# Keys and values of a token tile as one 1280-column product over three PSUM banks, with a block of MLP weights loaded ahead of later tokens and a longer estimate for late transposes

## The chip, the cores and the metric

The kernel runs on one core of one Trainium2 chip. The metric is the time of one execution in microseconds (us), measured on the device; lower is better. Several executions are timed, and medians with their ranges are given. The profile of one execution comes from the hardware profiler. Its span is shorter than the timed figure of the same run (266.6 against 268.37 us for the kernel before).

## The reference

A layer norm feeds two branches, and both are added to the input (S = 2048 tokens, D = 640, 32 heads of 20, F = 1536):

```
xn  = layernorm(x)
# A: linear attention; the features are softmax(p) and softmax(-p) over the 20 channels of a head
q, k, v = split(xn @ wqkv)
pq, pk  = q @ w_phi, k @ w_phi                      # per head
phi     = concat(softmax(p), softmax(-p))
o       = (phi_q @ (phi_k^T v)) / (phi_q . sum(phi_k) + 1e-6)
a       = o @ wo
# B: gated MLP
b       = (silu(xn @ w1) * (xn @ w3)) @ w2
out     = x + a + b
```

## The kernel before

Tokens stand in 16 tiles of 128. A scheduler written in Python runs while the program is built: each piece of work ("a product", "an evacuation", "a DMA") has an estimated duration; the pieces come from twelve streams; the piece that could start first goes next. So each engine gets one fixed order of instructions, made from estimates. The chip then runs each engine's list in order and waits on semaphores where the estimates were too optimistic. Any edit of a cost, or of a piece of work, can reorder everything that follows.

Three terms recur. Each matmul comes with a weight load (PEld in the profile) of its stationary tile, 128 x 128 values by which its columns are multiplied. Its result goes to PSUM, which the program treats as eight banks of 512 columns. An evacuation copies the result out of a bank, which frees the bank for the next product.

The key weights are first folded with w_phi (`fold_mm`), so that one product of xn gives the key features before the exponentials. V and K had a weight tensor each, and each product of a tile filled two banks of 320 columns:

```python
    Wkp = new("Wkp", [128, DC, D], bf, RKV)
    wv = new("wv", [128, DC, D], bf, RKV + 6400)
...
    def proj(t, w, k):
        for q in range(2):
            for i in range(DC):                      # DC = 5 blocks of 128 rows
                mm(bank(k + q, 320), xnT[:, i, t * 128:(t + 1) * 128],
                   w[:, i, 320 * q:320 * q + 320], i == 0, i == DC - 1)
...
    def v_tile(t, k):
        proj(t, wv, k)                               # then one ScalarE copy of 640 columns
...
    def k_features(t, k):
        proj(t, Wkp, k)                              # then two ScalarE exponentials of 640 columns
```

Of the first loads, these go out last, on one queue and in this order; `w13(a, b)` loads columns a to b of w1 and then of w3:

```python
        w13(0, 512)
        P.dma("SP", phi_s[:], phi_t)
        P.dma("SP", wqkT[:, DC:2 * DC, :], A_wqkv[:, D:2 * D], True)
        load_x(4, 8)
        load_x(8, 12)
        w13(512, 1024)
```

The scheduler's estimate of a DMA that transposes (`turn`), from its issue to its landing, ends with this line. After 80 us such transposes are those of the query features (tile `EqT`) and of the attention output (`oT`):

```python
                o.end = self.bus + (2.3 if turn and t > 80 else 1.6 if turn else 1.3 if t < 4.5 else 1.9)
```

The softmax here doesn't subtract the row's maximum and nothing guards it: scores larger than these inputs give would overflow.

## Time and profile before

| | before |
|---|---|
| time, median of 3 | 268.77 us (268.58 to 268.81) |
| span of the profiled run | 266.6 us |
| TensorE (PE) busy | 262.1 us, 1951 matmuls |
| VectorE, ScalarE, GpSimd busy | 182.9, 107.4, 95.6 us |
| PE stalls over 30 ns, after the start-up | 0.55 us at 23.5 us and 0.20 us at 125.7 us |

From the page of the profile: each engine's busy time with its share of the span and its count of instructions; the share of each of 40 slices in which PE is busy; the granted clock of PE in the same slices, in tenths (9 is 90% or more); and the chain of work that ended last.

```profile
span 266.6 us, 4819 instructions
...
PE 262.1 (98%) x1951; PEld 162.1 (61%) x1951; DVE 182.9 (69%) x312; ACT 107.4 (40%) x227; POOL 95.6 (36%) x107
...
PE   7999999999999999999999999999999999999996
...
PEclk9999999999999999999999999999999999999999
...
PE PS L104 90%; SPq L116 5%; DMA w_s<-in_B_w_dram 4%; DVE xres L104 0%
```

PE bounds the kernel. The chain, though, is not PE throughout: 4% of the span is a load of MLP weights. (The profile drops buffer numbers: `w_s` is w1 or w3, and w2.) In order of time (start, duration; "issue" is a moment in which nothing visible is waited for), the load is followed by PE to nearly the end:

```profile
14.78 9.38 DMA w_s<-in_B_w_dram
24.15 0.14 issue
24.29 101.68 PE PS L104 x839
125.97 0.04 issue
126.00 138.34 PE PS L104 x968
```

The timeline of PE just there (start, duration, what ran, and in brackets the idle time before it) shows where the chain leaves PE:

```profile
22.66 1.24 PE L104 MATMUL PS<-xnT,w_s 128*128 128x512 bf16 x5
24.29 1.24 PE L104 MATMUL PS<-xnT,w_s 128*128 128x512 bf16 x5 [0.39 <-DMA w_s<-in_B_w_dram]
25.36 0.48 PE L104 MATMUL PS<-BDc,wqkT 128*128 128x140 bf16 x6
25.68 2.32 PE L104 MATMUL PS<-xnT,w_s 128*128 128x512 bf16 x10
```

Five matmuls on w1 run, and the five on w3 wait for their weights. The five would follow at 22.66 + 5 x 0.216 = 23.74 us; they start at 24.29. That is 0.55 us, more than the 0.39 in brackets, because the end of a matmul is modelled with its pipeline behind it. For the same reason I measure PE by the distance from one matmul's start to the next one's. It was 216 ns at 512 columns, 136 at 320 and 56 at 128, which is columns/2.4 plus 2.7 ns by these medians; whatever is left over by 30 ns or more I call a stall. (Some matmul records are missing from a trace. Such a hole shows as exactly one matmul's time too much and is not counted.)

The waits by pair (who waited for whom, in total us, number, longest) name both stalls of the table, the first seen on PE and the second on its weight loads:

```profile
PE PS L104 <- DMA w_s<-in_B_w_dram: 0.4, 1, 0.4
PEld PS L104 <- DMA EqT<-eqt: 0.4, 1, 0.4
```

Groups by shape (count, busy us, mean ns of one, idle before). The product changed here is the last two lines:

```profile
L104 PE MATMUL PS<-xnT,w_s 128*128 128x512 bf16 x480 | 108.6, 379 | 0.4 <-DMA w_s<-in_B_w_dram 0.4
...
L104 PE MATMUL PS<-wv,xnT 128*128 128x320 bf16 x160 | 24.4, 299 | 0.1
L104 PE MATMUL PS<-Wkp,xnT 128*128 128x320 bf16 x160 | 23.9, 299 | 0.0
```

And the stage in which V and K are made (stretch, then its length and the busy time of PE, weight loads, DVE, ACT and POOL, each with its count; then the granted clock, the DMA engines' share and their GB/s): the other engines are 83% busy or more, but PE has no gap.

```profile
27.80:76.10 48.30, 48.30 (x351) 32.86 (x350) 45.38 (x72) 41.59 (x62) 40.17 (x44) 1.00 0.48 110
```

### The profile page before, as it was taken

What the parts mean: (1) busy time and instruction counts of PE and PEld (TensorE: products, weight loads), DVE (VectorE), ACT (ScalarE), POOL (GpSimd) and SP (SyncE); (2) the same over time, 40 slices, a digit from 0 to 9 for tenths busy, and PEclk for the clock granted to TensorE, in tenths of its full rate; (3) what the DMA queues carried; (4) which work ended last, traced back from release to release, by engine and by line L of the source; (5) the groups of instructions that cost most, each with busy time, mean ns of one, the idle gap of its engine ahead of it and who ended that gap; (6) DMA issues with size and microseconds to landing.
All of it is one profiled execution on the core that took longest, in us unless ns stands there. A gap on an engine that the chain in (4) does not pass through costs nothing.

```text
span 266.6 us, 4819 instructions
## 1 busy us (share of the span) xinstructions
PE 262.1 (98%) x1951; PEld 162.1 (61%) x1951; DVE 182.9 (69%) x312; ACT 107.4 (40%) x227; POOL 95.6 (36%) x107
## 2 busy tenths in 40 slices
PE   7999999999999999999999999999999999999996
PEld 3754666766766756556465655466565746777773
DVE  4567899999777497778767677969775857212112
ACT  5546688898871325332251314451414220000000
POOL 4211289898999032522207030617030430000000
PEclk9999999999999999999999999999999999999999
DMA  7996045962400773619503543061825074331211
GB/s 223 277 316 173 1 105 108 324 85 49 125 0 2 188 247 72 131 28 130 128 0 70 114 85 69 10 128 35 148 52 128 0 126 84 76 98 49 87 38 49
DMA packets 62742, 27.73 MB, mean 104 GB/s; under 512 B 49920, under 2 KB 62720, under 8 KB 62720
## 3 DMA queue, kind: packets, MB, share of 16 engines
q1 hardware_dynamic: 62576, 27.26, 44.4%
q8 instruction: 15, 0.25, 0.4%
q10 hardware_dynamic: 144, 0.16, 0.2%
q14 instruction: 7, 0.06, 0.1%
HBM read 12.81 MB, written 2.62 MB: 58 GB/s over the span
## 4 chain that ended last, share of the span: by engine, by line
PE 90%; SPq 5%; DMA 4%; issue 0%; DVE 0%
PE PS L104 90%; SPq L116 5%; DMA w_s<-in_B_w_dram 4%; DVE xres L104 0%
## 5 line engine op out<-in xcount | busy, mean ns | idle before, releaser
L104 PE MATMUL PS<-xnT,w_s 128*128 128x512 bf16 x480 | 108.6, 379 | 0.4 <-DMA w_s<-in_B_w_dram 0.4
L104 PEld LDWEIGHTS PS<-xnT,w_s 128*128 128x128 bf16 x480 | 46.2, 98 | 51.3 <-DVE Wkp L104 0.9
L104 POOL TENSOR_TENSOR eqt<-eqt,rS 128x600 bf16<-128x600 bf16 (+1 forms) x32 | 41.0, 1304 | 90.8 <-DVE rS L104 90.8
L104 ACT ACTIVATE th<-PS 128x512 f32<-128x512 f32 x48 | 28.6, 595 | 74.0 <-PE PS L104 73.9
L104 PE MATMUL PS<-w_s,hT 128*128 128x320 bf16 (+2 forms) x384 | 54.9, 299 | 0.0
L104 DVE SCALAR_TENSOR_TENSOR t<-th,PS 128x512 bf16<-128x512 f32 x48 | 32.5, 677 | 31.6 <-ACT th L104 31.5
L104 PEld LDWEIGHTS PS<-w_s,hT 128*128 128x128 bf16 x384 | 37.1, 98 | 15.1
L104 POOL TENSOR_TENSOR ekt<-ekt,rS 128x640 bf16<-128x640 bf16 x32 | 39.7, 1273 | 3.9 <-DVE rS L104 3.9
L104 ACT ACTIVATE eqt<-PS 128x240 bf16<-128x240 f32 (+1 forms) x96 | 27.2, 348 | 26.0 <-PE PS L104 24.1
L104 DVE TENSOR_TENSOR xres<-PS,xres 128x640 bf16<-128x640 f32 (+2 forms) x17 | 13.3, 782 | 34.6 <-PE PS L104 34.6
L104 DVE SCALAR_TENSOR_TENSOR hT<-t,PS 128x512 bf16<-128x512 bf16 x48 | 33.0, 687 | 2.0 <-PE PS L104 0.4
L104 ACT ACTIVATE ekt<-PS 128x640 bf16<-128x640 f32 x32 | 22.3, 703 | 7.0 <-PE PS L104 6.4
L104 DVE TENSOR_REDUCE S<-ekt 128x64 f32<-128x1280 bf16 x16 | 23.2, 1452 | 2.2 <-ACT ekt L104 2.2
L104 PE MATMUL PS<-wo_s,oT 128*128 128x320 bf16 (+2 forms) x160 | 24.5, 299 | 0.0
L104 PE MATMUL PS<-wv,xnT 128*128 128x320 bf16 x160 | 24.4, 299 | 0.1
L104 PE MATMUL PS<-Wqp,xnT 128*128 128x360 bf16 (+1 forms) x160 | 24.3, 299 | 0.0
L104 DVE TENSOR_REDUCE S<-eqt 128x66 f32<-128x1320 bf16 x16 | 24.2, 1513 | 0.0
L104 PE MATMUL PS<-Wkp,xnT 128*128 128x320 bf16 x160 | 23.9, 299 | 0.0
L104 PEld LDWEIGHTS PS<-Wqp,xnT 128*128 128x128 bf16 x160 | 15.2, 98 | 7.6
L104 PEld LDWEIGHTS PS<-wv,xnT 128*128 128x128 bf16 x160 | 15.4, 98 | 6.4 <-ACT xnT L104 0.3
L104 PEld LDWEIGHTS PS<-Wkp,xnT 128*128 128x128 bf16 x160 | 15.4, 98 | 6.1
L104 PEld LDWEIGHTS PS<-wo_s,oT 128*128 128x128 bf16 x160 | 15.3, 98 | 6.0
(52 smaller groups left out, 156.7 us busy)
## 6 DMA issues: line engine op xcount, KB each, us to landing
w_s<-in_B_w_dram SPq DMA_DIRECT2D x6, 640.0 KB, 7.2
xres<-in_A_x_dram SPq DMA_DIRECT2D x16, 160.0 KB, 2.5
out_dram<-xres SPq DMA_DIRECT2D x15, 160.0 KB, 1.8
x_tok<-in_A_x_dram SPq DMA_DIRECT2D x3, 640.0 KB, 4.5
w_s<-in_B_w_dram SPq DMA_DIRECT2D x1, 1920.0 KB, 8.8
wo_s<-in_A_wo_dram SPq DMA_DIRECT2D x1, 800.0 KB, 4.7
wv<-in_A_wqkv_dram SPq DMA_DIRECT2D x2, 320.0 KB, 4.3
x_tok<-in_A_x_dram SPq DMA_DIRECT2D x3, 160.0 KB, 2.6
```

Of the source, the lines that this page charges most:

```text
L104: o = _Op(eng, lambda: m(*args, **kw), r, w, cost)
L116: o = _Op(eng, lambda: m(out, in_), self.regions(in_), self.regions(out), nbytes, True)
```

## The change

The intent is fewer matmuls for the same columns, and MLP weights in time. V and K weights become one tensor of 1280 columns. For tiles 4 to 15 the product is cut at bank limits, 512, 512 and 256: 15 matmuls in place of 20. Tiles 0 to 3 have their V early and keep a product for K alone, now 512 + 128. A piece of work may now take any run of free banks, not only an aligned pair. Columns 512 to 1023 of w1 and w3 go ahead of x tiles 8 to 11. And the scheduler's estimate for late transposes grows by 0.4 us.

```diff
-                o.end = self.bus + (2.3 if turn and t > 80 else ...)
+                o.end = self.bus + (2.7 if turn and t > 80 else ...)
...
-    Wkp = new("Wkp", [128, DC, D], bf, RKV)
-    wv = new("wv", [128, DC, D], bf, RKV + 6400)
+    WVK = new("WVK", [128, DC, 2 * D], bf, RKV)
...
         load_x(4, 8)
+        w13(512, 1024)
         load_x(8, 12)
-        w13(512, 1024)
...
     def k_features(t, k):
-        proj(t, Wkp, k)
+        for q, lo, hi in ((0, 0, 512), (1, 512, D)):
+            for i in range(DC):
+                mm(bank(k + q, hi - lo), xnT[...], WVK[:, i, D + lo:D + hi], i == 0, i == DC - 1)
+        k_exps(t, 512 * k)
+
+    def vk_features(t, k):
+        for q, lo, hi in ((0, 0, 512), (1, 512, 1024), (2, 1024, 2 * D)):
+            for i in range(DC):
+                mm(bank(k + q, hi - lo), xnT[...], WVK[:, i, lo:hi], i == 0, i == DC - 1)
+        act(v2[...], PS[:, 512 * k:512 * k + D]..., ACT.Copy)
+        k_exps(t, 512 * k + D)
...
-        return min(range(0, 8, n), key=free_at)
+        return min(range(0, 9 - n), key=free_at)
...
-            yield lambda t=t: k_features(t, banks(2))
...
-            if t >= 4:
-                yield v(t)
...
+            if t < 4:
+                yield lambda t=t: k_features(t, banks(2))
+            else:
+                yield lambda t=t: vk_features(t, banks(3))
```

More of the change, by code (lines that the diff above doesn't have):

```diff
@@ L182, in commit @@
                 self.bus = max(self.bus, t + 0.5) + o.cost / rate
-                o.end = self.bus + (2.3 if turn and t > 80 else 1.6 if turn else 1.3 if t < 4.5 else 1.9)
+                o.end = self.bus + (2.7 if turn and t > 80 else 1.6 if turn else 1.3 if t < 4.5 else 1.9)
             else:
@@ L419, in first_loads @@
         for a, b in ((0, 2), (2, 4), (4, DC)):
-            P.dma("SP", wv[:, a:b, :], wqkv_t[:, a:b, 2 * D:3 * D])
+            P.dma("SP", WVK[:, a:b, 0:D], wqkv_t[:, a:b, 2 * D:3 * D])
         load_x(3, 4)
@@ L533, in fold_mm @@
                     first[q] = False
-        dst = (Wqp, Wkp)[which]
-        evac(dst[:, dc, :].rearrange("p (b c) -> p b c", c=320), bank2(k, 320))
-    def proj(t, w, k):
-        for q in range(2):
-            for i in range(DC):
-                mm(bank(k + q, 320), xnT[:, i, t * 128:(t + 1) * 128],
-                   w[:, i, 320 * q:320 * q + 320], i == 0, i == DC - 1)
+        dst = Wqp[:, dc, :] if which == 0 else WVK[:, dc, D:2 * D]
+        evac(dst.rearrange("p (b c) -> p b c", c=320), bank2(k, 320))
     def v_out(t, q, k):
@@ L552, in v_half @@
         for i in range(lo, hi):
-            mm(bank(k, 320), xnT[:, i, t * 128:(t + 1) * 128], wv[:, i, 320 * q:320 * q + 320],
+            mm(bank(k, 320), xnT[:, i, t * 128:(t + 1) * 128], WVK[:, i, 320 * q:320 * q + 320],
                i == 0, i == DC - 1)
@@ L560, in v_first @@
             for q in range(2):
-                mm(bank(k + q, 320), xnT[:, i, 0:128], wv[:, i, 320 * q:320 * q + 320], i == 0, i == DC - 1)
+                mm(bank(k + q, 320), xnT[:, i, 0:128], WVK[:, i, 320 * q:320 * q + 320], i == 0, i == DC - 1)
         if hi == DC:
@@ L564, in v_first, with k_exps @@
             v_out(0, 1, k + 1)
-    def v_tile(t, k):
-        proj(t, wv, k)
-        pv = bank2(k, 320).rearrange("p b (h c) -> p b h c", c=DH)
-        act(v2[:, t, :].rearrange("p (b h c) -> p b h c", b=2, c=21)[:, :, :, 0:DH], pv, ACT.Copy)
-    def k_features(t, k):
-        proj(t, Wkp, k)
-        o = ekt[:, t, :].rearrange("p (b h s f) -> p b h s f", b=2, s=2, f=DH)
-        for sg in range(2):
-            act(o[:, :, :, sg, :], bank2(k, 320).rearrange("p b (h f) -> p b h f", f=DH), ACT.Exp,
-                1.0 if sg == 0 else -1.0)
+    def k_exps(t, c):
+        o = ekt[:, t, :].rearrange("p (h s f) -> p h s f", s=2, f=DH)
+        i = PS[:, c:c + D].rearrange("p (h f) -> p h f", f=DH)
+        for sg in range(2):
+            act(o[:, :, sg, :], i, ACT.Exp, 1.0 if sg == 0 else -1.0)
+    def k_features(t, k):
+        for q, lo, hi in ((0, 0, 512), (1, 512, D)):
+            for i in range(DC):
+                mm(bank(k + q, hi - lo), xnT[:, i, t * 128:(t + 1) * 128], WVK[:, i, D + lo:D + hi],
+                   i == 0, i == DC - 1)
+        k_exps(t, 512 * k)
+    def vk_features(t, k):
+        for q, lo, hi in ((0, 0, 512), (1, 512, 1024), (2, 1024, 2 * D)):
+            for i in range(DC):
+                mm(bank(k + q, hi - lo), xnT[:, i, t * 128:(t + 1) * 128], WVK[:, i, lo:hi], i == 0, i == DC - 1)
+        act(v2[:, t, :].rearrange("p (h c) -> p h c", c=21)[:, :, 0:DH],
+            PS[:, 512 * k:512 * k + D].rearrange("p (h c) -> p h c", c=DH), ACT.Copy)
+        k_exps(t, 512 * k + D)
     def q_features(t, k):
@@ L813, in attention @@
     def attention():
-        def v(t):
-            return lambda: v_tile(t, banks(2))
         yield warm_up
@@ L832, in attention @@
                 yield None
-            yield lambda t=t: k_features(t, banks(2))
-            done["k"] = t + 1
-            if t >= 4:
-                yield v(t)
-            done["v"] = t + 1
+            if t < 4:
+                yield lambda t=t: k_features(t, banks(2))
+            else:
+                yield lambda t=t: vk_features(t, banks(3))
+            done["k"] = done["v"] = t + 1
             if 9 <= t < 14:
```

## The prediction

> **What bounds the kernel.** TensorE. The page gives PE 262.1 of 266.6 us busy (98%), the granted clock is 1.00 in every stretch, and the chain of waits is PE work from 24.29 us to the last output tile (two PE pieces, 101.7 and 138.3 us). VectorE (183), ScalarE (107) and GpSimd (96) have slack over the whole span. In the V/K stage (27.8 to 76.1 us, view of busy time by stretch) they do not: DVE 45.4, ACT 41.6, POOL 40.2 of 48.3 us; but PE is still busy for all 48.30, because MLP products fill its gaps.
>
> Inside PE, I take start-to-start distances of successive matmuls: 512 columns 216 ns, 320 columns 136, 128 columns 56. That is columns/2.4 GHz plus 2.5 to 2.7 ns, as the Trainium skill's page "TensorE: Matmul & The Clock Gate" (section "Wait — 56ns, not 53.3ns?") has it; a new stationary tile for every matmul costs nothing more. All columns together take 254.0 us at 2.4 GHz; the small overheads sum to 5.3 us over 1951 matmuls. All other PE loss after the first 7 us is two stalls: 0.55 us at 23.5 us (waiting for w3 columns 512-1023, which land at 24.15, behind x tiles 8-11, which land at 19.37) and 0.20 us at 125.7 us (a transposed query tile, EqT).
>
> **What the change does.**
> 1. V and K of tiles 4-15: 20 matmuls of 320 columns become 15 (512, 512, 256). Columns are unchanged. Five fewer per tile, 12 tiles: 60 x 2.65 ns = 0.16 us. PE time of a tile goes from 2.72 us to 2.70.
> 2. K of tiles 0-3 as 512+128 in place of 320+320: same count and columns, nothing.
> 3. Evacuation: the same three ScalarE instructions of 640 columns per tile (0.71 + 2 x 0.72 us). They now come as one 2.15 us group after one product, over three banks. The middle bank is held longer; 3 + 3 + 2 banks still let a second V/K product or an MLP pair run. Nothing on balance, with a small risk of a stall.
> 4. The load order: w1/w3 columns 512-1023 go ahead of 640 KB of x. From the landings 17.58 (x 4-7), 19.37 (x 8-11), 22.43, 24.15 us, w3 should land about 1.8 us earlier, near 22.3, and the stall of 0.55 us goes. x tiles 8-11 land near 24; their statistics start at 34.9, so that is free.
> 5. The scheduling model assumes DMA transposes after 80 us land 0.4 us later. The query stage is then ordered differently; the 0.20 us stall at 125.7 may go (I count 0.1).
>
> All of 1, 4 and 5 are on the critical path, as PE is. Sum: -0.16 - 0.55 - 0.1 = -0.8 us. The order of the whole program after 20 us is recomputed, so I allow +0.15 us for new short stalls. The first 20 us and the tail (last matmul at 264.1, then add and store) do not change.
>
> **Predicted: 268.1 us**, 267.5 to 269.1 (8 in 10). Faster by over 2%: 0.01; within 2%: 0.97; slower by over 2%: 0.02.
>
> **What would show it.** (1) 1891 matmuls, V/K groups with 512 and 256 columns at 216 and 109 ns. (4) No PE gap near 23.5 us; w3's second load landing near 22.3. (3) PE still fully busy from 28 to 76 us. (5) No PE wait on EqT. PE busy near 262 us and a span near 265.9.
>
> **What would make it wrong.** The V/K stage turning ScalarE-bound: the three-bank group held up by ScalarE, PE stalling for a bank; a new order of the query stage with DMA waits on EqT or oT; or K's later evacuation delaying the last key normalisation, so that the K-V sum starts late and PE runs out of MLP work.

## The result and the profile after

| | before | after |
|---|---|---|
| time, median of 6 | 268.79 us (268.20 to 269.00) | 267.64 us (267.37 to 268.11) |
| ratio, after to before | | 0.9962 (95%: 0.9949 to 0.9975) |
| span of the profiled run | 266.6 us | 265.9 us |
| PE busy, matmuls | 262.1 us, 1951 | 262.1 us, 1891 |

A ratio here is the mean time of one kernel's fast runs over that of the other's fast runs of the same rounds, so it is not quite the ratio of the medians. It says 0.38% faster, about 1.0 us; the predicted gain was 0.7 us, and 267.64 lies inside the predicted 267.5 to 269.1.

From the page of the changed kernel, the lines that answer to those of before:

```profile
span 265.9 us, 4695 instructions
...
PE 262.1 (99%) x1891; PEld 155.9 (59%) x1891; DVE 183.9 (69%) x313; ACT 106.3 (40%) x226; POOL 95.9 (36%) x107
...
PE   7999999999999999999999999999999999999996
...
PE PS L104 96%; DMA x_tok<-in_A_x_dram 1%; DVE bst L104 1%; DVE x_tok L104 0%; DVE mv L104 0%; POOL rstd L104 0%; DVE xres L104 0%
```

(This page has no row of the clock; 512-column matmuls were 216 ns apart, as before.) The load of MLP weights is gone from the chain, which is now PE from the start-up to the end. Note what does not show the gain: PE was busy for 262.1 us before and is busy for 262.1 us after, and its row of 40 slices is the same digit for digit. That equality is partly chance: in the first 20 us PE was busy for 18.22 us before and 18.56 after, and from there on for 243.91 and 243.56. The Trainium skill, on the page "Trainium Kernel Development and Optimization" (section "Performance Expectations"), calls matmul busy time a bad metric for how close a kernel is to roofline (the peak rate), because matmuls are pipelined. Here, too, it misled: 0.7 us of span went, and the sum of busy time did not move.

PE's timeline at the place of the first stall (the two groups of five are now one group of ten, without idle time before it):

```profile
22.31 0.60 PE L104 MATMUL PS<-BDc,wqkT 128*128 128x140 bf16 x8
22.75 2.32 PE L104 MATMUL PS<-xnT,w_s 128*128 128x512 bf16 x10
24.90 0.48 PE L104 MATMUL PS<-BDc,wqkT 128*128 128x140 bf16 x6
25.22 2.99 PE L104 MATMUL PS<-WVK,xnT 128*128 128x512 bf16 x20
```

The second w3 load landed at 24.15 us before and lands at 22.93 now. The groups by shape show the new product: 140 matmuls of 512 columns (20 of them for K alone, tiles 0 to 3) and 60 of 256, 216 and 109 ns apart.

```profile
L104 PE MATMUL PS<-xnT,w_s 128*128 128x512 bf16 x480 | 108.2, 379 | 0.0
...
L104 PE MATMUL PS<-WVK,xnT 128*128 128x512 bf16 x140 | 32.9, 379 | 0.0
...
L104 PE MATMUL PS<-WVK,xnT 128*128 128x256 bf16 x60 | 8.5, 273 | 0.0
```

The V/K stage is as full as before, with 58 matmuls fewer in the same stretch, and the waits by pair hold no DMA on EqT. One new wait is on the fold of the key weights:

```profile
27.80:76.10 48.30, 48.30 (x293) 26.49 (x292) 44.57 (x69) 41.64 (x64) 41.96 (x47) 1.00 0.47 110
```

```profile
PEld PS L104 <- ACT WVK L104: 0.4, 1, 0.4
```

(The first fence is the view of busy time by stretch, the second the view of waits.) On PE that wait costs 0.10 us, at 25.87 us: the first K product is reached before the fold of the last 128 rows is out of PSUM.

### The profile page after: what moved, and what is told of

It is laid out like the page before. It is cut to its first block, busy times and chain, and to the rows that moved or that the text cites. A ratio compares the mean times of both kernels' runs of the same rounds, so it can differ in the third digit from the quotient of the medians.

```text
span 265.9 us, 4695 instructions
## 1 busy us (share of the span) xinstructions
PE 262.1 (99%) x1891; PEld 155.9 (59%) x1891; DVE 183.9 (69%) x313; ACT 106.3 (40%) x226; POOL 95.9 (36%) x107
## 4 chain that ended last, share of the span: by engine, by line
PE 96%; DVE 1%; DMA 1%; POOL 0%; issue 0%
PE PS L104 96%; DMA x_tok<-in_A_x_dram 1%; DVE bst L104 1%; DVE x_tok L104 0%; DVE mv L104 0%; POOL rstd L104 0%; DVE xres L104 0%
## 5 line engine op out<-in xcount | busy, mean ns | idle before, releaser
L104 PE MATMUL PS<-WVK,xnT 128*128 128x512 bf16 (+3 forms) x260 | 45.6, 330 | 0.1
L104 PEld LDWEIGHTS PS<-WVK,xnT 128*128 128x128 bf16 x260 | 24.2, 98 | 19.4 <-ACT WVK L104 0.4
L104 ACT ACTIVATE ekt<-PS 128x640 bf16<-128x640 f32 x32 | 22.3, 703 | 1.3 <-PE PS L104 0.8
L104 DVE RECIPROCAL rS<-S 128x64 f32<-128x64 f32 (+1 forms) x32 | 17.9, 560 | 1.1
L104 DVE TENSOR_TENSOR o_tok<-PS,g_s 128x360 bf16<-128x360 f32 (+1 forms) x32 | 15.7, 491 | 1.1
```

The lines of the kernel that those rows point to most:

```text
L104: o = _Op(eng, lambda: m(*args, **kw), r, w, cost)
```

## The experiments

**How the traces are compared.** Every program here has the same work up to the last of the twenty TensorE transposes of the start-up, and that comes at 10.65 to 13.72 us, depending on the run. So I take PE from the start of that transpose to the start of the last matmul, and subtract the stalls of 30 ns or more found in between. What stays is the base: columns plus the fixed cost of each matmul, plus waits too short to count.

Theory "stalls": the gain is a smaller base (fewer matmuls) plus named PE stalls that went. Rival "product": the three-bank product itself is worth more than its 60 matmuls, or the stalls are absorbed later. Rival "reordering": a luckier order of the whole program.

**1. Load order alone** (kernel before; no compute instruction changes place).

```diff
         load_x(4, 8)
+        w13(512, 1024)
         load_x(8, 12)
-        w13(512, 1024)
```

> The kernel before with only the load order changed (MLP columns 512-1023 ahead of x tiles 8-11); the order of every compute engine's instructions is unchanged. Theory 'stalls' (the gain is the removal of named PE stalls): the 0.55 us stall near 23.5 us goes, the 0.20 us wait on EqT near 125 us stays, 1951 matmuls stay; 0.55 us faster than before, near 268.2 us. Rival 'product' (the gain is the three-bank product, the stall is absorbed later): the stall goes but time stays within 0.2 us of before.

Measured: 268.62 us (267.83 to 270.05), ratio 1.0005 (0.9979 to 1.0031). The time expected, 0.55 us faster and near 268.2 us, did not come; the interval is 0.7 us wide to each side and just holds it, so timing neither confirms nor excludes it. The trace is clearer: w3 lands at 22.52 us, there is no stall near 23.5 us, one of 0.12 us on EqT at 125.2 us is left, and the base is that of before (table below). PE has no idle time where the stall was:

```profile
22.75 2.32 PE L104 MATMUL PS<-xnT,w_s 128*128 128x512 bf16 x10
```

**2. Load order alone put back** (changed kernel; again no compute instruction changes place).

> The changed kernel with only the load order put back; the order of the compute engines' instructions is that of the changed kernel. Theory 'stalls': the stall near 23.5 us comes back at 0.5 to 0.6 us and time rises by 0.55 us over the changed kernel, near 268.2 us. Rival 'product': the stall is absorbed, within 0.2 us of the changed kernel.

Measured: 268.35 us (267.55 to 269.01) beside 267.81 for the changed kernel. The medians differ by 0.54 us, as expected, but the ranges overlap, and so do the ratios to before, 0.9978 (0.9953 to 1.0003) and 0.9959 (0.9938 to 0.9980). The profiled run shows a stall of only 0.10 us: w3 landed at 24.30, while PE itself was late, with the last start-up transpose at 11.28 us in place of 10.67. The stall is the difference of two moving times. That was not expected, so the trace of this run does not confirm the stall of 0.5 to 0.6 us.

**3. The load made later** (kernel before).

```diff
         load_x(8, 12)
+        load_x(12, 16)
+        P.pending[-1].cost = 0      # not seen by the scheduler, so that the order is kept
         w13(512, 1024)
```

> The kernel before with 640 KB more ahead of the MLP columns 512-1023: x tiles 12-15 are loaded once before them (and again later, as before, with the same data); the order of all compute instructions is kept. Theory 'stalls': the load's lateness passes one to one into PE time: w1 and w3 land about 1.8 us later, the stall near 23.5 us grows from 0.55 to 2.0 to 2.6 us and time by 1.5 to 2.1 us over before. Rival 'absorbed': later stages have room, time grows by less than half of that.

Measured: 270.53 us (269.72 to 271.11), ratio 1.0060 (1.0030 to 1.0089), 1.7 us over the median before. PE's timeline:

```profile
22.59 0.79 PE L104 MATMUL PS<-BDc,wqkT 128*128 128x140 bf16 x12
24.54 1.24 PE L104 MATMUL PS<-xnT,w_s 128*128 128x512 bf16 x5 [1.16 <-DVE Wkp L104]
26.29 1.24 PE L104 MATMUL PS<-xnT,w_s 128*128 128x512 bf16 x5 [0.51 <-DMA w_s<-in_B_w_dram]
```

The two gaps cost 1.33 and 0.68 us of start-to-start distance, 2.00 in all, at the lower end of the 2.0 to 2.6 expected. (The first is put down to DVE, which had long been done; the w1 load landed at 24.41 us, 0.13 before the start.) Lateness of this load passes into the time; nothing later absorbs it.

**4. The product alone** (load order and estimate as before).

> The kernel before with only the 1280-column product and its three-bank allocation; old load order, old 2.3 us assumption for late transposes. Theory 'stalls': 60 matmuls fewer save 0.16 us; the stall near 23.5 us stays at 0.55 us (order up to there is the same); the order made with 2.3 us plans waits on EqT near 111, 171 and 192 us, which I expect at 0.2 to 1.0 us in all on the chip; net between 0.1 us faster and 0.7 us slower than before. Rival 'product': 0.5 us or more faster than before.

Measured: 269.36 us (268.35 to 270.38), ratio 1.0031 (1.0007 to 1.0054): slower than before. The rival "product" falls. The profiled run, with 268.35 us the fastest of the six, had no stall on w3 (it landed at 23.30 us) but one of 0.77 us on EqT at 190.8 us:

```profile
188.87 2.32 PE L104 MATMUL PS<-xnT,w_s 128*128 128x512 bf16 x10
191.79 0.48 PE L104 MATMUL PS<-KVc,EqT 128*128 128x63 bf16 x11 [0.60 <-DMA EqT<-eqt]
```

The planned waits at 111 and 171 us did not show.

**5. The changed kernel with the old estimate for late transposes.**

```diff
-                o.end = self.bus + (2.7 if turn and t > 80 else ...)
+                o.end = self.bus + (2.3 if turn and t > 80 else ...)
```

> The changed kernel with the assumption for late transposes put back to 2.3 us: same product, same load order. Theory 'stalls': waits of PE on EqT come back near 111, 171 and 192 us, 0.2 to 1.0 us in all, so it is slower than the changed kernel by that much and near 268.0 to 268.6 us; no stall at 23.5 us. Rival 'the assumption does not matter': within 0.1 us of the changed kernel, no wait on EqT.

Measured: 268.75 us (268.49 to 270.38), ratio 1.0014 (0.9991 to 1.0036), so 0.9 to 1.1 us over the changed kernel's medians (267.81 and 267.64), about the upper end of the 0.2 to 1.0 us expected, and a little over the 268.0 to 268.6 us. The trace shows the cause, the same as in experiment 4:

```profile
189.53 2.32 PE L104 MATMUL PS<-xnT,w_s 128*128 128x512 bf16 x10
192.56 0.49 PE L104 MATMUL PS<-KVc,EqT 128*128 128x63 bf16 x11 [0.71 <-DMA EqT<-eqt]
```

The stall measures 0.88 us from start to start. With the larger estimate the order is another, and the traces of the changed kernel have no wait on EqT. One number of the diff decides whether the change gains 1.0 us or ties with before.

**6. That estimate alone** (kernel before).

> The kernel before with only the 2.7 us assumption for late DMA transposes, so the query stage is ordered anew. Theory 'stalls': stall near 23.5 us stays at 0.55; the 0.20 us wait on EqT goes or shrinks; 0.0 to 0.2 us faster than before. Rival 'reordering' (the new order of the query stage is what gained): 0.5 us or more faster.

Measured: 268.49 us (267.82 to 269.28), ratio 0.9993 (0.9973 to 1.0013): no difference resolved, though the interval still reaches a gain of 0.7 us. The trace speaks against "reordering": the base is that of before (252.68 us in the table below), and the wait on EqT, expected to shrink, is 0.20 us in this order too. And the profiled run had waits on both halves of the MLP load, 0.73 and 0.68 us, far over the 0.55 expected:

```profile
23.45 1.24 PE L104 MATMUL PS<-xnT,w_s 128*128 128x512 bf16 x5 [0.57 <-DMA w_s<-in_B_w_dram]
25.21 1.24 PE L104 MATMUL PS<-xnT,w_s 128*128 128x512 bf16 x5 [0.51 <-DMA w_s<-in_B_w_dram]
```

**7. Many more matmuls** (changed kernel; columns, banks, evacuations and the order of all other work kept).

```diff
-        for q, lo, hi in ((0, 0, 512), (1, 512, 1024), (2, 1024, 2 * D)):
+        for lo in range(0, 2 * D, 128):
             for i in range(DC):
-                mm(bank(k + q, hi - lo), xnT[...], WVK[:, i, lo:hi], i == 0, i == DC - 1)
+                mm(PS[:, 512 * k + lo:512 * k + lo + 128], xnT[...], WVK[:, i, lo:lo + 128],
+                   i == 0, i == DC - 1, cost=...)      # the same estimate per column as before
```

> The changed kernel with the 1280 columns of V and K of tiles 4-15 in ten pieces of 128 columns, 50 matmuls per tile in place of 15, 420 more in all; same banks, same evacuations, same order of all other instructions. Theory 'fixed cost per matmul of 2.65 ns': 420 x 2.65 = 1.1 us slower than the changed kernel, 128-column matmuls 56 ns apart. [...]

The expectation set this against a rival, "weight loads", by which a new stationary tile for each matmul sets the pace. One weight load takes 98 ns in the traces, so 600 matmuls would come 42 ns later each, 25 us in all (an estimate from these traces).

Measured: the base rises from 252.48 to 253.53 us, 1.05 us over 420 matmuls, 2.5 ns each. The matmuls of 128 columns of tiles 4 to 15 come 56 ns apart (597 distances, longest 56) although each has a new stationary tile. The rival "weight loads" falls.

```profile
L104 PE MATMUL PS<-WVK,xnT 128*128 128x128 bf16 x615 | 36.0, 219 | 0.0
```

(Groups by shape between 30 and 78 us.) Its time was 268.64 us; four of six runs lie between 268.49 and 268.67, 0.8 us over the changed kernel, and two at 270.7 and 270.9. The profiled run is one of those two. Its start-up matmuls ran at half speed (transposes 107 ns apart) until 10.16 us. The edit changes no matmul before 30 us, so it is not what made the start-up slow; the other slow run was not profiled.

**8. The kernel before, three more traces.** Because the stall on w3 came out so differently, before was profiled again.

> The kernel before, unchanged, for a second trace of it. Theory 'stalls': from the last of the first transposes to the last matmul PE takes 252.68 us plus its stalls, as in the first trace (253.44 with 0.55 and 0.20 us of stalls); the stall on w3 near 23.5 us is anywhere from 0 to 1.4 us, as in the four traces with the old load order. Rival: the base differs by more than 0.05 us from trace to trace, and the sums made from it mean nothing.

> The kernel before, unchanged, for a third trace. Theory 'stalls': base 252.68 us within 0.03; a stall on the second w1/w3 load in some of the traces, from 0 to 1.4 us, with its size set by the landing of that load against the time at which PE reaches it. With 0.55 and 0 so far, the mean over four traces of this kernel should be 0.3 to 0.8 us if it is to carry the timed difference of 1.0 us together with 0.2 us of base and 0.1 us of waits on EqT. Rival: no stall in these two, and the timed difference lies elsewhere.

> The kernel before, unchanged, for a fourth trace: as for the third.

Measured: 268.18, 268.36 and 269.08 us, one run each, their state unknown for want of more. The stalls on w1/w3 are 0, 0.57 and 0.89 us; with the first trace's 0.55 the mean is 0.50, within the 0.3 to 0.8 us asked for, and the base is the same within 0.03 us, so both rivals fall. Of the fourth trace:

```profile
22.88 1.24 PE L104 MATMUL PS<-xnT,w_s 128*128 128x512 bf16 x5
24.69 1.24 PE L104 MATMUL PS<-xnT,w_s 128*128 128x512 bf16 x5 [0.56 <-DMA w_s<-in_B_w_dram]
```

**9. The changed kernel again, and its last stall taken out.** The repeat of the changed kernel is the yardstick for experiments 2 and 7.

> The changed kernel itself, for a comparison on the same chip as the other runs of this call: 1.0 us faster than before, 267.7 us.

Measured: 267.81 us (267.49 to 267.99), ratio 0.9959 (0.9938 to 0.9980). Then the one stall left, 0.10 us before the first K product, was removed: in that one product the two matmuls on the last 128 rows of the folded weights come last.

```diff
-        for q, lo, hi in ((0, 0, 512), (1, 512, D)):
-            for i in range(DC):
...
+        parts = [(q, lo, hi, i) for q, lo, hi in ((0, 0, 512), (1, 512, D)) for i in range(DC)]
+        if t == 0:
+            parts.sort(key=lambda p: p[3] == DC - 1)
+        for q, lo, hi, i in parts:
...
+        if t == 0:
+            P.pending[-1].cost += 0.1093
```

> The changed kernel with the key product of token tile 0 reordered: its two matmuls on the last 128 rows of the folded key weights come last, after the other eight; the order of all other work is kept. Theory 'stalls': the changed kernel's one stall left, 0.10 us at 25.8 us, goes; from the last of the first transposes to the last matmul PE takes 252.48 us against 252.58; the time stays within 0.2 us of the changed kernel, as 0.1 us is below what timing resolves. Rival: the stall only moves to a later matmul, and the 252.58 us stay.

Measured: 267.69 us (267.46 to 270.44), ratio 0.9967 (0.9949 to 0.9985). The trace has no stall at all after the start-up, and 252.48 us from transpose to last matmul, the forecast value. In time it ties with the changed kernel. (Its profiled run, 270.44 us, is the slowest of seven, for a reason in the start-up that the last section shows; the stretch measured here comes after it.) (The last two lines of the diff correct the scheduler's estimate by 0.11 us, which keeps the order of all else.)

**All traces in one table.** "From transpose" is the time from the last start-up transpose to the last matmul; stalls are those of 30 ns or more.

| kernel | from transpose, us | stall on w1/w3 | on EqT | on the fold | base |
|---|---|---|---|---|---|
| before | 253.44 | 0.55 | 0.20 | 0 | 252.69 |
| before, second trace | 252.82 | 0 | 0.12 | 0 | 252.70 |
| before, third | 253.46 | 0.57 | 0.18 | 0 | 252.71 |
| before, fourth | 254.07 | 0.89 | 0.49 | 0 | 252.69 |
| load order alone | 252.81 | 0 | 0.12 | 0 | 252.69 |
| estimate alone | 254.30 | 1.41 | 0.20 | 0 | 252.68 |
| load made later | 254.80 | 2.00 | 0.12 | 0 | 252.68 |
| product alone | 253.35 | 0 | 0.77 | 0.10 | 252.49 |
| changed, old estimate | 253.47 | 0 | 0.88 | 0.10 | 252.49 |
| changed, old load order | 252.67 | 0.10 | 0 | 0.10 | 252.48 |
| changed | 252.58 | 0 | 0 | 0.10 | 252.48 |
| changed, repeated | 252.58 | 0 | 0 | 0.10 | 252.48 |
| changed, last stall out | 252.48 | 0 | 0 | 0 | 252.48 |
| changed, pieces of 128 | 253.63 | 0 | 0 | 0.10 | 253.53 |

Apart from the last row, with its 420 matmuls more, there are two bases, to within 0.03 us: 252.7 for 1951 matmuls and 252.5 for 1891. Everything else is a named stall. And the stall on w1/w3 follows from two readings of each trace: PE starts the waiting matmul 0.13 to 0.15 us after the weights land, or when it gets there, whichever is later.

| trace with the old load order | w3 lands | PE gets there | PE starts | stall on w3 |
|---|---|---|---|---|
| before | 24.15 | 23.74 | 24.29 | 0.55 |
| before, second | 23.78 | 24.17 | 24.17 | 0 |
| before, third | 24.14 | 23.72 | 24.28 | 0.57 |
| before, fourth (0.16 us on w1 besides) | 24.55 | 23.96 | 24.69 | 0.73 |
| estimate alone (0.73 us on w1 besides) | 25.07 | 24.53 | 25.21 | 0.68 |
| product alone | 23.30 | 23.81 | 23.81 | 0 |
| changed, old load order | 24.30 | 24.34 | 24.44 | 0.10 |

("Gets there" is worked out from the start of the matmul before it plus 0.216 us.) With the new order w3 landed at 22.33 to 22.93 us in the four traces whose last start-up transpose came by 11.41 us, and it held PE up in none of the six traces that have that order.

## Why the prediction was right

The predicted time held: 268.1 us (267.5 to 269.1), measured 267.64 and 267.81. Term by term, with the mean of the four traces of before against the two of the changed kernel:

| term | predicted, us | measured, us |
|---|---|---|
| fewer matmuls (1) | -0.16 | -0.22 (base 252.70 to 252.48) |
| stall on w1/w3 (4) | -0.55 | -0.50 (mean of 0.55, 0, 0.57, 0.89) |
| waits on EqT (5) | -0.1 | -0.25 (mean of 0.20, 0.12, 0.18, 0.49) |
| new stalls | +0.15 | +0.10 |
| sum | -0.66 | -0.87 (253.45 to 252.58) |

- **What bounds the kernel.** Right. Since PE has no slack after the start-up, each term appeared one to one; experiment 3 shows it for a delay of 2.0 us.
- **Step 1, the matmuls.** Right in kind and close in size. Experiment 7 puts the fixed cost at 2.5 ns, so 60 matmuls are 0.15 us. The other 0.07 us of base is four short waits of PE near 59 and 67 us in the trace of before (24, 13, 24 and 14 ns of overhead where 2.6 is usual, 65 ns in all); the changed order has none there. The trace puts two of the four down to a ScalarE exponential of K that frees a bank. Step 3 had called the evacuation neutral; it seems to have gained these few hundredths.
- **Step 2, K of tiles 0 to 3 costs nothing.** Wrong by 0.10 us. The count is the same, but in the new order no MLP product stands between the last fold and the first K product, so PE reaches the last folded rows too early. Both the product alone and the whole change have this stall; load order alone does not. The allowance for new stalls covered it. Why the scheduler picks that order was not tested.
- **Step 4, the load order.** Right by the traces, and the largest single term; in time alone it was not resolved (experiment 1 shows no gain, experiment 2 one of 0.54 us with overlapping ranges). Its size was read from one trace, and that was partly luck: over the four traces of before the stall is 0 to 0.89 us, 0.50 on average. The landing near 22.3 us was forecast; it was 22.93 and 22.33. What I did not foresee is that the stall depends on two moving times, the landing and the start-up. Without it the time should be steadier, but the runs do not show that: twelve timed runs of the changed kernel lie within 0.74 us (267.37 to 268.11) and eleven of before in one call within 1.97 us (267.81 to 269.78), yet six of before in the call of the result lie within 0.80 us, and six with the load order alone, whose trace has no such stall either, within 2.22 us (267.83 to 270.05). Slow start-ups, as in experiments 7 and 9, hit the new order too.
- **Step 5, the estimate.** Mis-sized. I counted 0.1 us for the stall that I could see in the kernel before. Against before the waits fell by 0.25, but only together with the new product (the estimate alone left a wait of 0.20, experiment 6). Within this change the estimate is worth 0.9 us, because the order that the new product brings has a wait on EqT of its own (0.77 and 0.88 us in experiments 4 and 5). Without it, the change would have been a tie or a loss.
- **Failure modes named.** None came in the full change; a query stage with DMA waits on EqT did come in experiments 4 and 5.

The 0.87 us of the traces lies within both intervals of the timed difference (0.67 to 1.37 and 0.5 to 1.7 us, from the ratios).

## What to carry to other kernels

Where one engine is full, a small edit is worth its fixed costs plus the stalls that it removes or makes, and the second part can be the larger: here 60 matmuls were 0.15 us, and the waits on two kinds of DMA landing were five times that, 0.50 and 0.25 us. Measure such a gain from start to start on that engine, from a point after the start-up, and count stalls by name; what is left of two traces then agrees within 0.03 us, where timed runs differ by 1 us. A stall read from one trace is a sample: profile the unchanged kernel more than once before you put a number on it, and test a change of a scheduler's estimate together with the change whose order it protects.

## What the Trainium skill lacked or had wrong

- "TensorE: Matmul & The Clock Gate", section "Back-to-back issue gap", gives a sustained 81 ns per matmul at N = 128 and 131 ns at N = 512 for a stream of weight loads and matmuls. Here, with a new stationary tile for every matmul, it was 56 ns (597 distances, none longer) and 216 ns. The formula N/2.4 + 2.5 ns, which that section calls the isolated gap, is the one that holds in the stream.
- The same page, section "LDWEIGHTS (loading the stationary operand)", gives P/1.2, so 107 ns for 128 columns. The profile of before shows 95 to 99 ns (median 98) for all but 11 of 1951 loads, and these loads fit under matmuls 56 ns apart.
- The same page, section "What's actually happening", has the clock go cold by default or after at least one idle window. In the trace of the kernel with its last stall out, the clock of PE came up at 5.49 us; PE was busy for 1.80 of the 3.41 us from there on, its longest idle stretch being 1.27 us, and still the next 3.42 us ran at half clock. Its time, 270.44 us, is 2.8 us over that kernel's median. A stretch in which PE was half busy was enough. In the nine other traces that record when the clock came up, PE was busy for 2.10 to 3.41 us of the first 3.41 us after that, and the clock stayed. No page gives a busy share at which the clock falls. The view of busy time by stretch (the clock is the third number from the end):

```profile
5.49:8.90 3.41, 1.80 (x16) 1.03 (x17) 1.82 (x6) 1.59 (x4) 1.11 (x2) 1.00 0.96 322
8.90:12.32 3.42, 3.42 (x18) 2.17 (x17) 1.32 (x4) 1.47 (x4) 0.55 (x1) 0.50 1.53 273
```

- "DMA: Bandwidth & Descriptors" has no figure for the spread of one transfer's landing between executions of one program. Here the second w3 load landed at 23.78 to 24.55 us in four traces of the same kernel; and the sixteen transposes of one tensor, alike in size, took 3.5 to 5.2 us from issue to landing in one trace (median 3.7).
